# Row sums of a fused attention and feed-forward kernel moved directly behind the value product, with one more warm-up matmul

## The chip, the cores and the metric

One core of one Trainium2 chip. The metric is the device time of one execution in microseconds (us), a median over runs. The kernel before takes 463.5 us (three runs, 463.35 to 464.38). TensorE multiplies matrices into PSUM, ScalarE computes exponentials and other functions, VectorE does elementwise arithmetic, GpSimd prepares inputs and issues loads, SyncE issues transposing transfers and stores. Single executions scatter: 35 runs of the kernel before in one set lay between 461.23 and 467.68 us. So most numbers below are durations inside a profile, and whole times are compared over many runs.

## The reference

Attention over 8 batches, 12 heads, 448 positions and 64 columns, followed by a gated feed-forward block over 3584 tokens:

```python
scores = scale * np.matmul(q, k.transpose(0, 1, 3, 2))
scores = scores - np.max(scores, axis=-1, keepdims=True)
attn = np.exp(scores)
attn = attn / (np.sum(attn, axis=-1, keepdims=True) + 1e-09)
x = np.matmul(attn, v)          # -> (3584, 768)
g = x @ w_gate                  # (768, 1536)
silu = g * (1.0 / (1.0 + np.exp(-g)))
out = silu * (x @ w_val) @ w_out
```

## The kernel before

It works through the heads in pairs and weaves attention and feed-forward into **visits**. A visit computes three score chunks of a pair (`s`), one or two products of an earlier pair of pairs (`acc`: the row sums, or one half of the value product), the small last score chunk (`sr`), and then a share of the feed-forward work of an earlier batch (`gp` and `vp`, a gate and a value projection; `op`, the output projection). A PSUM buffer is free again when its **reader**, the engine that takes the result out, is done. Every `acc`, `sr`, `vp` and `op` takes its PSUM buffer from one pool, `ps_f`, of **two** buffers, in turn; `s` and `gp` take theirs from `ps_s`, with three.

```python
ps_s = ctx.enter_context(tc.tile_pool(name="ps_s", bufs=3, space=PSUM))
ps_f = ctx.enter_context(tc.tile_pool(name="ps_f", bufs=2, space=PSUM))
...
def scaled(p0, t, acc):                     # reader of a value product
    ...
    nc.vector.tensor_tensor(X[kk][...], acc[:, 0:S], R[p0][:], ALU.mult)

def sums(p0, wide=False):                   # row sums: E times a matrix of ones
    if wide:
        acc = ps_s.tile([128, 2, 512], FP32, tag="s", name="acc")[:, 0]
    else:
        acc = ps_f.tile([128, 512], FP32, tag="f", name="acc")
    ...
def recips(p0, acc):                        # reader of the row sums
    ...
    nc.vector.tensor_copy(ssb[:], acc[:, 0:S])
    return [...]                            # four reciprocals, issued later one by one
...
def mm(dst, lhsT, rhs, start, stop):        # feed-forward matmul
    if not tiled[0]:
        nc.tensor.matmul(dst, lhsT=lhsT, rhs=rhs, start=start, stop=stop)
        return
    for j in range(4):                      # four pieces of 32 columns: the form of the products
        nc.tensor.matmul(dst[ts(j, 32), :], lhsT=lhsT[:, ts(j, 32)], rhs=rhs, ...)
...
def product(kind, p0):
    if kind == "sums":
        pop_deferred(99)
        deferred.extend(recips(p0, sums(p0)))
    else:
        pop_deferred(99)
        scaled(p0, kind, pv(p0, kind))
```

In the loop over visits, `todo` holds up to two products. Where it holds two, the first is the second half of a value product and the second the row sums of the next pair of pairs. The first is issued behind the scores; the sums come behind `sr` (early blocks) or behind the visit's `gp`,`vp` pairs (later blocks), except in a visit that opens a new block, where both come together.

The softmax here doesn't subtract the row's maximum and nothing guards it: scores larger than these inputs give would overflow.

Of the kernel before, what the change touches and what calls it, by code (L numbers as in the profile page):

```python
# [23 lines left out]
TILED = 8  # L24
# [4 lines left out]
def kernel(  # L29
# [72 lines left out]
    def dummy(n):  # L102
        wp = ps_f.tile([128, 512], FP32, tag="f", name="wp")
        for _ in range(n):
            nc.tensor.matmul(wp[:], lhsT=warm[:, 0:128], rhs=warm[:], start=True, stop=True)
# [40 lines left out]
    def load_v(g):  # L146
        b = g // GPB
        heads = ds((g % GPB) * 2 * GP, 2 * GP)
        v16[g] = raws.tile([128, 2 * GP * NC * D], FP16, tag="vt", bufs=3, name="vt")
        if g * GP < FULL:  # L150
            nc.gpsimd.dma_start(v_old(g), v[b, heads].rearrange("h (p c) d -> p h (c d)", c=NC))
            return
        nc.gpsimd.memset(v_rest(g), 0.0)  # L153
        nc.gpsimd.dma_start(v_main(g), v[b, heads, 0:SM].rearrange("h (p c) d -> p h (c d)", c=3))
        for hx in range(2):
            nc.gpsimd.dma_start(
                v_rest(g)[ts(hx, SR), :, hx],
                v[b, heads, SM:].rearrange("(i t) p d -> t p i d", t=2)[hx],
            )
# [14 lines left out]
    def prep(pr):  # L174
        if pr >= FULL:
            rq, km, kr = raw[pr]
            qk16 = attp.tile([128, 2, NC, 2, D], FP16, tag="qk16", bufs=3, name="qk16")
            nc.gpsimd.memset(qk16[96:128, 1], 0.0)
            nc.gpsimd.memset(qk16[:, 0, 3], 0.0)
            nc.gpsimd.tensor_copy(qk16[:, 0, 0:3].rearrange("p c h d -> p h c d"), km)  # L180
            for hx in range(2):
                nc.gpsimd.tensor_copy(qk16[ts(hx, SR), 0, 3, hx], kr[ts(hx, SR)])
            nc.gpsimd.tensor_copy(qk16[0:P, 1].rearrange("p c h d -> p h c d"), rq)
            qkT[pr] = attp.tile([128, 2 * NC, 128], FP16, tag="qkT", name="qkT", bufs=5)
            nc.sync.dma_start_transpose(
                qkT[pr][:], qk16[:].rearrange("p t c h d -> p (t c h d)")
            )
            return None
        rq, rk = raw[pr]
        if pr == 0 or pr >= NPE:  # L190
            qk16 = attp.tile([128, 2, NC, 2, D], FP16, tag="qk16", bufs=3, name="qk16")[0:P]
            for t, src in enumerate((rq, rk)):
                dst = qk16[:, 1 - t].rearrange("p c h d -> p h c d")
                if pr == 0:
                    nc.vector.tensor_copy(dst[:, 0], src[:, 0])
                    nc.scalar.activation(dst[:, 1], src[:, 1], AF.Copy)
                else:
                    nc.gpsimd.tensor_copy(dst, src)
        qkT[pr] = attp.tile([128, 2 * NC, 128], FP16, tag="qkT", name="qkT", bufs=5)
        qkT[pr] = qkT[pr][:].rearrange("p c q -> p (c q)")[:, 0 : 2 * NC * P].rearrange(  # L200
            "p (c q) -> p c q", q=P
        )
        if pr >= NPE:
            nc.sync.dma_start_transpose(
                qkT[pr], qk16.rearrange("p t c h d -> p (t c h d)")
            )
            return None

        def turn0():
            for t in range(2):  # L210
                tp = ps_s.tile([128, 2, 512], FP32, tag="s", name="tp")
                for c in range(NC):
                    for hx in range(2):
                        nc.tensor.matmul(
                            tp[ts(hx, 64), c // 2, ds(c % 2 * P, P)],
                            lhsT=qk16[:, 1 - t, c, hx],
                            rhs=ident[:],
                            start=True,
                            stop=True,
                        )  # L220
                dst = qkT[pr][:, ts(1 - t, NC)].rearrange("p (a c) q -> p a (c q)", a=2)
                nc.vector.tensor_copy(dst[:, 0], tp[:, 0, 0 : 2 * P])
                nc.scalar.activation(dst[:, 1], tp[:, 1, 0 : 2 * P], AF.Copy)

        def turn():
            if pr < FIRST + 2:
                tp = ps_s.tile([128, 2 * NC, 256], FP16, tag="s", name="tp")
            else:
                tp = ps_f.tile([128, 2 * NC, 128], FP16, tag="f", name="tp")
            for t in range(2):  # L230
                for c in range(NC):
                    for hx in range(2):
                        src = raw[pr][t][:, hx, c, :]
                        nc.tensor.transpose(tp[ts(hx, 64), (1 - t) * NC + c, 0:P], src, ident[:])
            nc.vector.tensor_copy(qkT[pr], tp[:, :, 0:P])

        return turn if pr else turn0
# [92 lines left out]
    def recips(p0, acc):  # L330
        ssb = attp.tile([128, S], FP32, tag="ssb", bufs=1)
        nc.vector.tensor_copy(ssb[:], acc[:, 0:S])
        rt = R[p0]
        return [
            lambda i=i: nc.vector.reciprocal(rt[:, ts(i, P)], ssb[:, ts(i, P)]) for i in range(4)  # L335
        ]
# [6 lines left out]
    tiled = [False]  # L343
# [94 lines left out]
    with tc.manual_schedule():  # L438
# [10 lines left out]
        load_qk16(4)  # L449
        load_v(0)  # L450
        load_v(1)
        dummy(6)
        prep(0)()
        dummy(1)
        turn = prep(1)
# [21 lines left out]
        def pop_deferred(n=1):  # L477
            for _ in range(n):
                if deferred:
                    deferred.pop(0)()  # L480
# [82 lines left out]
        for p0 in range(FIRST, NPAIR, 2):  # L563
            x = done[p0 + 1] + 1
            step = 2 if x < len(visits) and len(visits[x]) == 2 else 1
            queue += [(x, "sums", p0), (x + step, 0, p0), (x + step + 1, 1, p0)]
        while len(plan) < len(visits) or queue:
            x = len(plan)
            todo = []
# [3 lines left out]
        adds = {0: 0}  # L573
# [5 lines left out]
# [8 lines that stand above are left out]
        carry = 0.0  # L587
        for x, (chunks, todo) in enumerate(plan):
            for pr, c in chunks:
                qk(pr, c)  # L590
            end = min([y for y in adds if y > x] + [len(plan) + 1])
            if x == 0:
                for t in range(2):
                    scaled(p4, t, halves[t])
                add_block(0, end)
            turn2 = None
            entered = [pr for pr, c in chunks if c == 0]
            for pr in entered:
                if NPE <= pr + 3 < NPAIR:
                    prep(pr + 3)  # L600
                if pr % 2 == 0 and 14 <= pr + LA < NPAIR:
                    load_qk16(pr + LA)
            for pr, c in chunks:
                if c == 2 and pr < NPE - 2:
                    prep(pr + 2)()
            if x in adds and x > 0:
                while todo:
                    product(*todo.pop(0)[1:])
                add_block(adds[x], end - x)
            elif todo:  # L610
                product(*todo[0][1:])
            for pr in entered:
                if (pr + 2) % GP == GP - 1 and 4 <= (pr + 2) // GP + 1 < NGRP:
                    load_v((pr + 2) // GP + 1)
                for w in wq.pop(pr, []):
                    emit(w)
            tiled[0] = bool(todo or x in adds) and (not chunks or chunks[0][0] >= TILED)
            for pr in entered:
                if pr >= FULL:
                    qk_rest(pr)  # L620
            if adds[max(y for y in adds if y <= x)] < 2:
                for item in todo[1:]:
                    product(*item[1:])
                carry = run_budget(left() / (end - x) + carry)
            else:
                at, n = count["at"], count["visits"]
                no = share(count["o"], at, n)
                nf = 1
                if no and count["more"] > 0:
                    o_left = sum(1 for y in range(at, n) if share(count["o"], y, n))  # L630
                    extra = -(-count["more"] // o_left)
                    nf += extra
                    count["more"] -= extra
                count["at"] += 1
                for y in range(nf):
                    if fvq:
                        run_fv()
                for item in todo[1:]:
                    product(*item[1:])
                for _ in range(no):  # L640
                    run_o()
            tiled[0] = False
# [36 lines left out]
```

## Time and profile before

| | before |
|---|---|
| median of three runs | 463.49 us |
| span of the profiled run | 463.2 us |
| TensorE busy | 97% |
| VectorE, ScalarE, GpSimd busy | 52%, 49%, 40% |
| groups of row sums | 24, of which 13 stand late (12 in visits, 1 in the tail) and are what the change moves |

In the lines of the profile, `E` are the exponentials, `ones` the matrix of ones, `X` a finished value product, `ssb` VectorE's copy of the row sums, `sg`, `t` and `hts` the steps from `gp` and `vp` to the input of `op`, and `wp` the warm-up matmuls, whose results nobody reads. A form such as `128*32` is the part of TensorE's array that one matmul uses (rows by columns); going from one form to another is a change of the tiling mode. An "issue" hole is idle time for which the profile shows no wait.

The prediction below shows the shares, TensorE's waits and a late visit of the later blocks. Two more views matter. The first is TensorE's timeline in an early block (start us, duration us, engine, line, operation, result<-operands, forms, count, and in brackets the idle time before with its releaser):

```profile
99.56 0.94 PE L284 MATMUL acc<-E,vt 128*32 128x448 f16 x16
100.33 0.36 PE L350 MATMUL sr<-qkT 128*32 128x448 f16 x4
101.24 0.94 PE L284 MATMUL acc<-E,ones 128*32 128x448 f16 x16 [0.54 <-DVE X L311]
...
107.29 0.78 PE L260 MATMUL s<-qkT 64*128 64x448 f16 x6
```

With two buffers, the third user in a row needs the buffer of the first: the sums wait until VectorE has read the value product (`X`). The second view is VectorE in the late visit that the prediction shows:

```profile
207.83 0.69 DVE L381 SCALAR_TENSOR_TENSOR hts<-t,vp 128x512 f16<-128x512 f32 x1
208.46 0.62 DVE L332 COPY ssb<-acc 128x448 f32<-128x448 f32 x1
```

`hts`, the reader of the last `vp`, ends at 208.52, and `op`, which needs that `vp`'s buffer, starts at 208.57. That is the repeated hole of 0.16 us.

### The profile page before, as it was taken

To read this page: it belongs to the slowest core of one execution; us is meant where nothing else is said; L and a number is where in the kernel's file an instruction comes from. 1 tells how busy PE (TensorE), PEld (TensorE's weight loads), DVE (VectorE), ACT (ScalarE), POOL (GpSimd) and SP (SyncE) were. 2 spreads that over 40 slices of the span, in tenths; PEclk is the share of its full clock that TensorE was granted. 3 is DMA by queue.
4 is the path that set the end of the run, shared out by engine and by line. 5 is a ranking of instruction groups with operands and counts; after the bars stand their busy time and mean duration, and the time that the engine had idled before them with its cause. 6 is when DMAs were issued, how large, how long until landed. Compare 5 with 4: busy or idle time off the path is not lost.

```text
span 463.2 us, 17335 instructions
## 1 busy us (share of the span) xinstructions
PE 449.4 (97%) x7843; PEld 247.7 (53%) x7843; DVE 238.8 (52%) x375; ACT 225.9 (49%) x353; POOL 184.3 (40%) x380
## 2 busy tenths in 40 slices
PE   8899999999999999999998999999999999999996
PEld 3345555544456655555555656555556666544564
DVE  2665754557773653646645527446366366355200
ACT  5986666555546445444554464445544642222222
POOL 8454825996975064910849018450230000000000
PEclk9999999999999999999999999999999999999999
DMA  9999999999798638990859558963342101200133
GB/s 137 196 201 200 186 178 126 185 167 148 88 99 113 83 45 130 121 120 3 120 92 98 95 83 116 105 62 81 60 55 59 37 3 38 69 0 2 34 103 102
DMA packets 99146, 45.62 MB, mean 98 GB/s; under 512 B 69888, under 2 KB 95616, under 8 KB 99072
## 3 DMA queue, kind: packets, MB, share of 16 engines
q0 software_dynamic: 54848, 23.37, 42.6%
q1 hardware_dynamic: 44128, 21.09, 26.7%
q8 instruction: 61, 1.00, 0.9%
q14 instruction: 13, 0.11, 0.1%
q10 hardware_dynamic: 96, 0.05, 0.0%
HBM read 47.19 MB, written 11.01 MB: 126 GB/s over the span
## 4 chain that ended last, share of the span: by engine, by line
PE 88%; DVE 5%; ACT 3%; issue 1%; DMA 1%; SPq 0%; DVEq 0%; ACTq 0%
PE gp L350 18%; PE op L350 18%; PE vp L350 16%; PE acc L284 11%; PE s L260 7%; PE op L347 6%; PE gp L347 5%; PE vp L347 5%; ACT E L263 2%; DVE t L378 2%; PE sr L350 2%; DVE hts L381 1%; ACT sg L366 1%; DVE R L335 1%; DMA rk<-in_k_dram 1%
## 5 line engine op out<-in xcount | busy, mean ns | idle before, releaser
L263 ACT ACTIVATE E<-s 128x896 f16<-128x896 f32 (+1 forms) x156 | 131.5, 923 | 13.9 <-PE s L260 13.7
L378 DVE SCALAR_TENSOR_TENSOR t<-sg,gp 128x384 f32<-128x384 f32 (+1 forms) x96 | 59.0, 615 | 90.1 <-ACT sg L366 90.0
L350 PE MATMUL vp<-X,wv 128*32 128x384 f16 (+1 forms) x1824 | 99.5, 351 | 1.6 <-issue 1.6
L350 PE MATMUL gp<-X,wg 128*32 128x384 f16 (+1 forms) x1824 | 99.2, 351 | 0.0
L366 ACT ACTIVATE sg<-gp 128x384 f32<-128x384 f32 (+1 forms) x96 | 53.4, 557 | 89.2 <-PE gp L350 63.9
L411 ACT ACTIVATE osb<-op 128x384 f32<-128x384 f32 (+1 forms) x57 | 27.6, 484 | 126.9 <-PE op L350 103.1
L350 PE MATMUL op<-wo,hts 128*32 128x384 f16 x1968 | 86.6, 326 | 2.9 <-issue 0.9
L350 PEld LDWEIGHTS <-hts 128*32 128x32 f16 x1968 | 56.0, 97 | 30.9 <-issue 6.4
L335 DVE RECIPROCAL R<-ssb 128x112 f32<-128x112 f32 x92 | 71.4, 820 | 0.8
L350 PEld LDWEIGHTS <-wv 128*32 128x32 f16 x1824 | 50.3, 97 | 37.6 <-issue 2.5
L350 PEld LDWEIGHTS <-wg 128*32 128x32 f16 x1824 | 50.8, 97 | 34.7
L311 DVE TENSOR_TENSOR X<-acc,R 128x448 f16<-128x448 f32 x48 | 29.7, 624 | 73.2 <-PE acc L284 70.8
L381 DVE SCALAR_TENSOR_TENSOR hts<-t,vp 128x384 f16<-128x384 f32 (+1 forms) x96 | 59.6, 621 | 11.9 <-PE vp L350 1.3
L153 POOL MEMSET vt<- 128x384 f16 x12 | 5.0, 419 | 113.3 <-PE acc L284 113.3
L284 PE MATMUL acc<-E,vt 128*32 128x448 f16 (+1 forms) x768 | 45.2, 355 | 0.0
L260 PE MATMUL s<-qkT 64*128 64x448 f16 x312 | 41.8, 358 | 1.8 <-ACT E L263 1.3
L347 PE MATMUL op<-wo,hts 128*128 128x384 f16 (+1 forms) x192 | 29.6, 316 | 0.0
L284 PEld LDWEIGHTS <-vt 128*32 128x32 f16 (+1 forms) x768 | 16.8, 96 | 23.0 <-issue 14.7
L347 PE MATMUL gp<-X,wg 128*128 128x512 f16 (+1 forms) x120 | 26.7, 358 | 0.2 <-DVE t L378 0.2
L347 PE MATMUL vp<-X,wv 128*128 128x512 f16 (+1 forms) x120 | 26.6, 358 | 0.0
L260 PEld LDWEIGHTS <-qkT 64*128 64x128 f16 x312 | 12.0, 94 | 27.2 <-issue 21.8
L284 PE MATMUL acc<-E,ones 128*32 128x448 f16 (+1 forms) x384 | 22.6, 353 | 2.1 <-DVE X L311 1.7
(53 smaller groups left out, 325.7 us busy)
## 6 DMA issues: line engine op xcount, KB each, us to landing
q<-in_q_dram POOLq DMA_DIRECT2D x22, 224.0 KB, 5.8
k<-in_k_dram POOLq DMA_DIRECT2D x18, 192.0 KB, 6.6
vt<-in_v_dram POOLq DMA_DIRECT2D x12, 288.0 KB, 7.0
out_dram<-osb SPq DMA_DIRECT2D x7, 336.0 KB, 3.2
wg<-in_moe_w_gate_dram POOLq DMA_DIRECT2D x8, 288.0 KB, 11.1
wv<-in_moe_w_val_dram POOLq DMA_DIRECT2D x8, 288.0 KB, 11.4
wo<-in_moe_w_out_dram POOLq DMA_DIRECT2D x2, 1152.0 KB, 18.6
out_dram<-osb SPq DMA_DIRECT2D x8, 288.0 KB, 3.1
```

The costliest lines, as they stand in the source:

```text
L153: nc.gpsimd.memset(v_rest(g), 0.0)
L260: nc.tensor.matmul(s[:, hx, 0:S], lhsT=lhsT, rhs=rhs, start=True, stop=True)
L263: nc.scalar.activation(dst, s[0:m, :, 0:S], AF.Exp, scale=sm_scale)
L284: nc.tensor.matmul(acc[ts(j, 32), 0:S], lhsT=weights(pr, hx, c), rhs=rhs, start=(c == 0), stop=(c == NC - 1),)
L311: nc.vector.tensor_tensor(X[kk][:, hp + t, ts(bb, S)], acc[:, 0:S], R[p0][:], ALU.mult)
L335: lambda i=i: nc.vector.reciprocal(rt[:, ts(i, P)], ssb[:, ts(i, P)]) for i in range(4)
L347: nc.tensor.matmul(dst, lhsT=lhsT, rhs=rhs, start=start, stop=stop)
L350: nc.tensor.matmul(dst[ts(j, 32), :], lhsT=lhsT[:, ts(j, 32)], rhs=rhs, start=start, stop=stop)
L366: nc.scalar.activation(sg[:, 0:n], gp[:, 0:n], AF.Tanh, scale=0.5)
L378: nc.vector.scalar_tensor_tensor(t1[:, 0:n], sg[:, 0:n], 1.0, gp[:, 0:n], ALU.add, ALU.mult)
L381: nc.vector.scalar_tensor_tensor(hts[:, fb, 0:n], t1[:, 0:n], 0.5 * HS, vp[:, 0:n], ALU.mult, ALU.mult)
L411: nc.scalar.activation(osb[:, ds(m0, w)], op[:, 0:w], AF.Copy, scale=1.0 / HS)
```

## The change

The intent, as the words of the change have it: both products of a visit stand directly behind its scores, so that the switch from feed-forward matmuls to products and back happens once per visit; and TensorE gets a seventh warm-up matmul at the start, before its first transposes.

```diff
-        dummy(6)
+        dummy(7)
         prep(0)()
@@
+            any_p = len(todo)
             if x in adds and x > 0:
                 while todo:
                     product(*todo.pop(0)[1:])
                 add_block(adds[x], end - x)
-            elif todo:
-                product(*todo[0][1:])
+            while todo:
+                product(*todo.pop(0)[1:])
@@
-            tiled[0] = bool(todo or x in adds) and (not chunks or chunks[0][0] >= TILED)
+            tiled[0] = bool(any_p) and (not chunks or chunks[0][0] >= TILED)
@@
             if adds[max(y for y in adds if y <= x)] < 2:
-                for item in todo[1:]:
-                    product(*item[1:])
                 carry = run_budget(left() / (end - x) + carry)
@@
                     if fvq:
                         run_fv()
-                for item in todo[1:]:
-                    product(*item[1:])
                 for _ in range(no):
                     run_o()
```

## The prediction

> **What bounds the kernel now.** I read the page first: engine shares, the 40 slices, the chain that ended last.
>
> ```profile
> PE 449.4 (97%) x7843; PEld 247.7 (53%) x7843; DVE 238.8 (52%) x375; ACT 225.9 (49%) x353; POOL 184.3 (40%) x380
> ...
> PE   8899999999999999999998999999999999999996
> ...
> PE 88%; DVE 5%; ACT 3%; issue 1%; DMA 1%; SPq 0%; DVEq 0%; ACTq 0%
> ```
>
> TensorE is busy in every slice and holds 88% of the chain; the others are half idle. Except in the first 25 us, where ScalarE's exponentials run without a break from 9.48 us to 24.5 us, the time is the sum of the matmuls plus the small holes between them. So a reordering can only win or lose holes. TensorE's own waits name them:
>
> ```profile
> PE acc L284 <- DVE X L311: 1.7, 3, 0.6
> PE vp L350 <- issue: 1.6, 2, 1.3
> ...
> PE op L350 <- issue: 0.9, 1, 0.9
> PE op L350 <- DVE hts L381: 0.7, 4, 0.2
> ```
>
> The three waits of `acc` and the four of `op` each name a reader that had not emptied a PSUM buffer. I then read TensorE's timeline (start us, us, ...), visit by visit. Three consecutive visits of one block give the whole argument; a visit runs from one `s` to the next:
>
> ```profile
> 182.03 0.74 PE L260 MATMUL s<-qkT 64*128 64x448 f16 x6
> 182.70 0.94 PE L284 MATMUL acc<-E,vt 128*32 128x448 f16 x16
> 183.47 0.93 PE L284 MATMUL acc<-E,ones 128*32 128x448 f16 x16
> 184.37 0.37 PE L350 MATMUL sr<-qkT 128*32 128x448 f16 x4
> ...
> 191.81 0.74 PE L260 MATMUL s<-qkT 64*128 64x448 f16 x6
> ...
> 200.67 0.74 PE L260 MATMUL s<-qkT 64*128 64x448 f16 x6
> ...
> 206.18 1.47 PE L350 MATMUL vp<-X,wv 128*32 128x512 f16 x24
> 207.48 0.93 PE L284 MATMUL acc<-E,ones 128*32 128x448 f16 x16
> 208.57 2.13 PE L350 MATMUL op<-wo,hts 128*32 128x384 f16 x48 [0.16 <-DVE hts L381]
> 210.64 0.55 PE L260 MATMUL s<-qkT 64*128 64x448 f16 x4
> ```
>
> The first visit already has the order of the change: the value product, then the row sums (`acc<-E,ones`), then the rest. It takes 191.81-182.03 = 9.78 us. The second has no sums and takes 8.86 us. The third has the same work as the first, but its sums stand behind two `gp`,`vp` pairs: 210.64-200.67 = 9.97 us. So the early place costs 0.92 us and the late one 1.11 us. That comparison, made on the chip in the kernel before, is the core of the forecast.
>
> **What the Trainium skill says.** "Perfetto Trace Analysis", section Optimization Strategy (under Identifying Performance Opportunities), reads the same gap, repeated on the engine that should be saturated, as a possible lack of SBUF or PSUM for the next tile. The trace agrees: 0.16 us appears four times and 0.54 to 0.57 us three times. "TensorEngine Tiling (Array Packing)", section Key Properties, says that changing the tiling mode drains TensorE. If that were the gain, it would be nil here: products and, in these visits, the feed-forward matmuls all have the form 128*32; `vp` to sums starts 207.48-206.18 = 1.30 us apart, as `gp` to `vp` does (206.18-204.89 = 1.29). "TensorE: Matmul & The Clock Gate", Part 1, gives 426.7 ns for 512 columns on the cold array; the first warm-up loads follow each other at 0.42 to 0.43 us, which agrees. "Runtime: NRT & Kernel Launch", section Instruction fetch mechanics, says that instructions come in blocks of 256 (16 KiB) by DMA, mostly hidden; the page shows 61 packets, 1.00 MB, on the instruction queue, and 15,688 TensorE instructions / 256 = 61.3. I take the three "issue" holes (1.31, 0.88, 0.33 us, all inside a group or where no buffer was awaited) for late blocks, which is an inference.
>
> **The change part by part.** The listing of the changed program's order settles what moves. Apart from one matmul, TensorE's instructions are the same in number and form; ScalarE, GpSimd and SyncE keep their order. Of 24 sums groups, 13 move; the other 11 already stand directly behind the value product or belong to the first part. In every moved case it is the sums that come forward; no value product moves.
>
> 1. Four visits with 512 columns and 48 `op` (200.67, 219.50, 312.10, 330.93): 9.97 each now, 9.78 in the early order. Cause: the `f` buffers are two. Late, the sums take the buffer of the first `vp` and the first `op` needs that of the second, whose reader `hts` ends at 207.83+0.69 = 208.52; the sums fill only 0.75 us of that wait. Early, the two `op` candidates are free. Gain 4 x 0.19 = 0.76.
> 2. Five visits with 384 columns (145.69, 163.86, 256.06, 274.23, 365.85): for example 172.49-163.86 = 8.63, against 138.11-129.61 = 8.50 early. Gain 5 x 0.13 = 0.65.
> 3. Two visits of the block without `op` (98.89, 114.24): 107.29-98.89 = 8.40 and 122.66-114.24 = 8.42, against 91.43-83.61 = 7.82 early. Here the late order is value product, `sr`, sums, and the sums wait for the buffer whose reader X is only just starting. Early, the sums take the other buffer and their 0.75 us of matmuls cover most of X; `sr` waits about 0.13 us instead (183.47 to 184.37 is 0.90, where 0.77 is a group's usual pitch). Gain 2 x 0.59 = 1.18.
> 4. The visit at 71.66: sums wait 0.57 for X, then `op` 0.21 for `sr`'s exponential. Early, sums at 73.10, `sr` after X (73.35+0.62) at about 74.0; then `op` waits for the copy of the sums, which VectorE starts after X and ends at about 74.75. `op` at about 74.8 instead of 75.18: gain 0.4. A new wait eats part of it.
> 5. The tail, 384.67: `op` at 385.71 is 1.04 behind the sums' start, 0.75 being their work. Early gain 0.29.
>
> Sum of 1 to 5: 0.76+0.65+1.18+0.4+0.29 = 3.3 us. All of it lies on the path, since TensorE is the path from about 25 us on.
>
> 6. The seventh warm-up matmul: the first six finish streaming at 1.20+6x0.427 = 3.76; the seventh streams until 4.19. The first transposes start at 4.09, when VectorE's cast is ready, so they slip 0.1 us; but their second half waits for another input (the cast that starts at 4.50) until 4.85. Cost 0 to 0.1, which I put at +0.1. Warmth could pay, as `s` at 8.88 is still slow (four in 0.93) and those at 11.52 fast (two in 0.36); I choose nothing for it.
>
> 463.49 - 3.3 + 0.1 = 460.3 us.
>
> **The rivals.** (a) **VectorE becomes late.** Early sums bring a copy of 0.62 and four reciprocals of 0.82 between the `t` and `hts` of the two pairs: 3.9 us beside 2 x 1.38 = 2.8, so 6.7 us where two pairs take TensorE 4 x 1.30 = 5.2. If `vp`'s buffer were freed late, each of nine visits could lose 0.5 us: up to +4.5, ending at about 465. Against it: the visits at 129.61, 182.03, 238.33, 293.46 and 349.77 have just this order, and `gp`,`vp` step on there without a hole; the last reciprocal spills into the `op` stretch. (b) **Fewer mode changes**, the apparent intent: worth several us if each moved group had a drain at both ends; the pitches above speak against it. (c) **The warm-up turns the clock on a window earlier**: the exponentials wait 1.12 us before 9.48, of which perhaps 0.7 could go: 459.6. (d) **The gaps are hidden anyway**, because a freed TensorE waits for exponentials: ScalarE has idle stretches of 0.6 to 3.7 us in every such visit, so I see little of that; it would make 463.5. (e) **Late instruction blocks move**: the issue holes total 2.5 us[...]; +1 or -1.5.
>
> **Range and chances.** The counted gain rests on durations of the same sequence, so I trust it to about 0.7 us; fetch holes and start add about 1 us. The range is 458.8 to 462.6. A change of 2% is 9.3 us, three times what all counted holes hold, so within 2% gets 0.98, each side 0.01.
>
> **What would show it.** In the changed profile: the waits of `acc` for X gone; the four waits of `op` for `hts` gone; visits of 9.8, 8.5 and 7.8 us where 9.97, 8.63 and 8.4 stood; `sr` 0.90 behind the sums in 13 more visits; a wait of `op` for the copy of the sums in the visit at 71.66; VectorE's total unchanged. Wrong would be: waits of `vp` or `op` for `hts` or `ssb` in the moved visits (rival a), or other issue holes.

## The result

The changed kernel gives the right result. Its median is 460.97 us (four runs, 459.87 to 461.38) against 463.94 us for the kernel before beside it (four runs). The ratio is 0.9931, with a 95% interval of 0.9904 to 0.9957. Ratios here are the mean time of one kernel's fast runs over that of the other's fast runs of the same rounds, so not quite the ratio of the medians. Two repeats on other occasions gave 0.9931 and 0.9932.

The page of the changed kernel, the lines that answer to those of before (engine shares; TensorE's busy tenths; the chain that ended last):

```profile
PE 446.9 (97%) x7844; PEld 250.2 (54%) x7844; DVE 238.6 (52%) x375; ACT 226.8 (49%) x353; POOL 184.3 (40%) x380
...
PE   8899999999999999999999999899999999999996
...
PE 93%; DVE 3%; ACT 2%; issue 1%; DMA 1%; SPq 0%; DVEq 0%; ACTq 0%
```

The chain is TensorE's to 93% instead of 88%: the steps through VectorE and ScalarE fell from 8% to 5%. TensorE's waits:

```profile
PE op L350 <- issue: 2.6, 1, 2.6
...
PE vp L350 <- issue: 1.1, 1, 1.1
...
PE op L350 <- DVE ssb L332: 0.4, 1, 0.4
```

The three waits of `acc` for `X` and the four of `op` for `hts` no longer appear. The forecast wait for the copy of the sums is there, once. The "issue" holes have grown from 2.5 to 3.7 us. The visit that answers to the late one of before (200.67 there):

```profile
196.88 0.74 PE L260 MATMUL s<-qkT 64*128 64x448 f16 x6
197.55 0.94 PE L284 MATMUL acc<-E,vt 128*32 128x448 f16 x16
198.32 0.93 PE L284 MATMUL acc<-E,ones 128*32 128x448 f16 x16
199.22 0.37 PE L350 MATMUL sr<-qkT 128*32 128x448 f16 x4
...
203.29 1.48 PE L350 MATMUL vp<-X,wv 128*32 128x512 f16 x24
204.59 2.14 PE L350 MATMUL op<-wo,hts 128*32 128x384 f16 x48
206.66 0.74 PE L260 MATMUL s<-qkT 64*128 64x448 f16 x6
```

It takes 9.78 us, and `op` starts 1.30 us behind `vp` without a hole. Going through all visits from one `s` to the next, before against after, only the moved ones and those with an issue hole differ by more than 0.02 us:

| part of the run | before to after, us |
|---|---|
| start, up to 68.16 us of before | -1.48 |
| visit at 71.66 | -0.42 |
| two visits of the early block (98.89, 114.24) | -0.56, -0.57 |
| five visits with 384 columns | -0.14, -0.11, -0.13, -0.11, -0.14 |
| four visits with 512 columns | -0.19, -0.17, -0.19, -0.17 |
| tail, to the next value product | -0.27 |
| three visits with issue holes (91.43, 246.83, 282.86) | -0.52, -0.34, +1.85 |
| span 463.2 to 459.6 | -3.6 |

So this pair of profiles gained 3.17 us from the moved sums, 1.48 us at the start, which I had not counted, and gave 0.99 us back in holes whose waits the profile cannot name. Were the start and the holes parts of the change, or chance? Theory: the moved sums gain 3.2 us by PSUM buffers, and the rest is chance (theory C of the expectations). Rivals: the place behind the value product pays in itself, by fewer changes of the tiling mode; the seventh warm-up matmul makes TensorE fast earlier and pays for part of it (theory B); the new order makes the issue holes longer.

### The profile page after: what moved, and what is told of

Its sections match the earlier page's. It is cut to its first block, busy times and chain, and to the rows that moved or that the text cites. A ratio compares the mean times of both kernels' runs of the same rounds, so it can differ in the third digit from the quotient of the medians.

```text
span 459.6 us, 17337 instructions
## 1 busy us (share of the span) xinstructions
PE 446.9 (97%) x7844; PEld 250.2 (54%) x7844; DVE 238.6 (52%) x375; ACT 226.8 (49%) x353; POOL 184.3 (40%) x380
## 4 chain that ended last, share of the span: by engine, by line
PE 93%; DVE 3%; ACT 2%; issue 1%; DMA 1%; SPq 0%; DVEq 0%; ACTq 0%
PE vp L350 18%; PE gp L350 18%; PE op L350 18%; PE acc L284 13%; PE s L260 7%; PE op L347 6%; PE gp L347 5%; PE vp L347 5%; PE sr L350 2%; ACT E L263 1%; DVE R L335 1%; DMA rk<-in_k_dram 1%; PE tp L234 0%; DVE ssb L332 0%; DVE X L311 0%
## 5 line engine op out<-in xcount | busy, mean ns | idle before, releaser
L335 DVE RECIPROCAL R<-ssb 128x112 f32<-128x112 f32 x92 | 73.9, 831 | 0.8
L350 PEld LDWEIGHTS <-wv 128*32 128x32 f16 x1824 | 51.7, 97 | 35.2 <-issue 1.5
L350 PEld LDWEIGHTS <-wg 128*32 128x32 f16 x1824 | 51.9, 97 | 32.6
L347 PEld LDWEIGHTS <-hts 128*128 128x128 f16 x192 | 18.4, 98 | 11.1
```

The lines of the kernel that those rows point to most:

```text
L335: lambda i=i: nc.vector.reciprocal(rt[:, ts(i, P)], ssb[:, ts(i, P)]) for i in range(4)
```

## The experiments

### Each half of the change alone

The seventh warm-up matmul alone, on the kernel before:

```diff
-        dummy(6)
+        dummy(7)
```

> The kernel before with the seventh warm-up matmul and nothing else. Theory A (my prediction's term 6): no gain, 0 to +0.1 us, about 464. Theory B (the changed kernel's profile, where the matmuls are fast from about 5.2 us on and the work at 68 us stands 1.5 us earlier): [...]1.0 to 1.5 us faster, about 462.5, in all or nearly all runs. Theory C: [...]the runs scatter over 1.5 us for six and for seven matmuls alike and the means agree.

The new order alone, the changed kernel with `dummy(6)`:

> The changed order with six warm-up matmuls. Counting theory: the visits of the moved sums shorten by 0.11 to 0.19 (nine), 0.57 (two), 0.42 (one) and 0.29 (the tail), in all 3.2 us, so about 460.8 if the instruction holes are as in the kernel before. If the seventh matmul carries 1.5 us of the measured 3 us, this run gains only 1.5 to 2 us unless the holes differ (theory: the larger hole of the changed kernel, 2.60 against 0.88 us, comes with the order).

Measured, on one chip: warm-up alone 463.93 us median against 463.98, ratio 1.0003 (0.9981 to 1.0024). The order alone 462.69 us, ratio 0.9966 (0.9946 to 0.9987), which is 1.6 us faster. A second set of the same kernel, with the edit repeated in a later call, had this expectation:

> The changed order tiled with six warm-up matmuls, again, now on one chip with the changed kernel. It was 1.9 us faster than before at a clock of 0.998 or more where the visits count 3.2. Theory B: its missing 1.3 us are late clocks that six matmuls leave to chance; it is about 1 us slower than the changed kernel beside it. Theory C: equal to the changed kernel within the scatter of 1.2 us a run.

It gave 461.63 us, ratio 0.9942 (0.9922 to 0.9963). So the order alone is faster. Both means, 1.6 and 2.7 us, lie below the 3.2 us that its visits count, though only the first interval excludes 3.2, and though in the profiles the moved visits were as short as in the changed kernel (in the first, 7.83, 10.45, 9.78). The matmul alone shows no gain. Both repeats of the whole change gave more than the order alone:

> The changed kernel once more, for a second profile and more runs on the chip of the others. Counting theory: the visits repeat to 0.02 us (9.78, 8.50, 7.84), and only the start and the instruction holes differ; at a granted clock of 0.998 or more it is 2 to 3 us faster than before, as the changed order with six warm-up matmuls (1.9) within the noise. If the seventh matmul matters, it is over 1 us faster than that run was.

> The changed kernel beside the run with six warm-up matmuls. About 460.6, as twice before; Theory B puts it 1 us below that run, Theory C at the same time. A third profile of its instruction holes: at the same places (visits near 243 and 278) or none, of 0.2 to 2.6 us.

They gave 460.76 us, ratio 0.9931 (0.9906 to 0.9956), and 461.22 us, ratio 0.9932 (0.9910 to 0.9955). Two of the last kernel's 19 runs were far off (517.4 and 1618.5 us), were marked slow and do not count. One source of scatter can be set apart: in the first set of the order alone, 7 of 22 runs had a mean granted clock of 0.995 or 0.996 and were 2.1 us longer than the others, where the kernel before beside it had 3 of 35 such runs. Without such runs, the means are 1.9 and 2.8 us below the kernel before for the order alone, 3.3 us both times for the whole change, and 0.0 for the warm-up alone. Even so, the intervals of all runs overlap, and at this scatter the parts cannot be separated by time.

### Buffers or place: the sums in the other pool

Both orders, with one edit: the sums of the main loop take a buffer of `ps_s`.

```diff
-                deferred.extend(recips(p0, sums(p0)))
+                deferred.extend(recips(p0, sums(p0, True)))
```

The order of before:

> The order of before; only the PSUM buffer of the row sums is taken from the three-buffer pool of the scores, in the main loop. Buffer theory: the late place costs nothing by itself, the two-buffer pool does; each sums group then costs its 0.75 us of matmuls wherever it stands (visits of 9.97 become about 9.6, 8.63 become 8.35, 8.40 become 7.7), some 5 to 6 us faster than before, about 458.5. Position theory (being directly behind the value product is what pays, or a mode change): no change, about 463.9.

The order of the change:

> The changed order and the sums in the pool of the scores. Buffer theory: the wait of 0.13 to 0.17 us of the small score matmul behind the sums goes, in some 20 visits, 3 us faster than the changed kernel, about 457.8, and within 0.5 us (apart from the warm-up) of the run with the late order in that pool. If the exponentials free the score buffer too late, the sums wait instead, up to 0.3 us each, and it is no faster than the changed kernel. Position theory: as the changed kernel, about 461.

Measured, beside the same runs of before: late 459.29 us, ratio 0.9884 (0.9847 to 0.9921); early 457.63 us, ratio 0.9877 (0.9838 to 0.9917). A late visit in that pool:

```profile
198.08 0.74 PE L260 MATMUL s<-qkT 64*128 64x448 f16 x6
...
203.59 1.47 PE L350 MATMUL vp<-X,wv 128*32 128x512 f16 x24
204.88 0.93 PE L284 MATMUL acc<-E,ones 128*32 128x448 f16 x16
205.64 2.12 PE L350 MATMUL op<-wo,hts 128*32 128x384 f16 x48
207.70 0.55 PE L260 MATMUL s<-qkT 64*128 64x448 f16 x4
```

It takes 9.62 us, 0.76 more than one without sums (8.86), which is the sums' own work; `op` follows 0.76 us behind them. The same stretch with the early order in that pool:

```profile
197.39 0.94 PE L284 MATMUL acc<-E,ones 128*32 128x448 f16 x16
198.14 0.38 PE L350 MATMUL sr<-qkT 128*32 128x448 f16 x4
```

Here `sr` starts 0.75 us behind the sums instead of 0.90, and the visit takes 9.66 us. So, in the tiled kernel, where the sums stand no longer matters once they leave the pool of two: late is even 0.04 us a visit better. **What the moved sums gained was a better rotation through two buffers.** The place theory is out. The two medians alone would not show this, since the early kernel also has the seventh warm-up matmul; the visits do, and both profiles have the same fast start (see below). Against the changed kernel I had expected 3 us; the ratios, 0.9877 and 0.9931, are about 2.5 us apart. One new wait takes part of it: in the visit at about 61 us, the sums wait 0.6 us for an exponential that must free a score buffer (that visit took 6.15 us instead of 5.53).

### Without tiling: mode changes, and a quieter kernel

The feed-forward matmuls of all visits in one piece of 128 columns, so that each passage between them and the products changes the tiling mode:

```diff
-TILED = 8
+TILED = 99
```

The order of before, six warm-up matmuls:

> The order of before with the feed-forward matmuls of all visits in one piece of 128 columns instead of four of 32. Mode theory (what the change seems to be for): the sums behind the feed-forward pairs now stand between two changes of the tiling mode, so a late sums visit costs about 0.2 us more against a visit without sums than in the tiled kernel (1.11 becomes 1.3). Fetch theory: TensorE's instructions fall from 15,688 to about 7,000, some 27 blocks instead of 61, so the issue holes (1.2 to 3.7 us in the profiles so far) mostly go. Against before: the added changes cost about 0.1 us each, four per visit more, in some 30 visits, so up to 6 us slower, less 2 us of holes.

The changed order, seven:

> The changed order without the tiling. Mode theory: early sums share the mode changes of the value product, so the visits of the moved sums shorten by 0.2 us more than in the tiled kernels: nine by 0.3 to 0.4, and the whole gains 5 us on the late order untiled. If a change of mode costs nothing, the gain is the 3.2 us of the buffers again.

Late: 464.66 us, ratio 1.0013 (1.0000 to 1.0026). Early: 459.08 us, ratio 0.9901 (0.9875 to 0.9926). TensorE's timeline of a late visit, and then of the sums and `sr` in the early kernel:

```profile
201.55 0.74 PE L260 MATMUL s<-qkT 64*128 64x448 f16 x6
202.22 0.94 PE L284 MATMUL acc<-E,vt 128*32 128x448 f16 x16
203.09 0.36 PE L347 MATMUL sr<-qkT 128*128 128x448 f16 x1
...
207.18 1.46 PE L347 MATMUL vp<-X,wv 128*128 128x512 f16 x6
208.56 0.94 PE L284 MATMUL acc<-E,ones 128*32 128x448 f16 x16
209.54 2.11 PE L347 MATMUL op<-wo,hts 128*128 128x384 f16 x12
211.58 0.74 PE L260 MATMUL s<-qkT 64*128 64x448 f16 x6
```

```profile
199.12 0.93 PE L284 MATMUL acc<-E,ones 128*32 128x448 f16 x16
200.02 0.35 PE L347 MATMUL sr<-qkT 128*128 128x448 f16 x1
```

A visit without sums changes the mode once more than a tiled one, before `sr`, and takes 8.97 us instead of 8.86: that change costs 0.11 us where nothing hides it. (`sr` starts 0.87 us behind the value product, 0.77 in the tiled kernel. A visit with late sums changes the mode three times more; the four that I had expected everywhere were too many.) A moved visit gains 0.26 to 0.28 us (10.03 to 9.75) where it gained 0.17 to 0.19 tiled. I had expected 0.2 more; it is 0.09 more, and not by the two changes around the late sums. From `vp` to `op` the late visit takes 2.36 us here and 2.39 tiled: in both, `op` starts 0.05 us after `hts` ends (209.49 here, 208.52 there), so both changes lie inside that wait. Against a visit without sums, late sums cost 1.06 us here and 1.11 tiled, early ones 0.78 and 0.92, so the 0.09 us come from the early side: `sr` starts 0.90 us behind the sums with a mode change and without, so the change that every other visit pays for is hidden in the wait for a buffer. Over all moved visits the untiled order gains 3.97 us and 0.27 in the tail, 4.24 together. The intended saving, fewer switches, shows in neither kernel: tiled, there are none to save, and untiled, those around the late sums cost nothing beside the wait. What they would cost in the late order with the sums in the other pool was not run.

The instruction queue of the late kernel's page (packets, MB, share of 16 engines):

```profile
q8 instruction: 29, 0.48, 0.4%
```

It moves 29 packets, where the tiled kernels move 61, and no untiled profile has an issue hole of TensorE. The scatter falls with it: the six runs of the early order lie within 0.6 us. The last combination, early and untiled with the sums in the other pool:

> The changed order, sums in the pool of the scores, without tiling: the three effects together. If the holes go and a mode change costs about 0.1 us: 3 us faster than the changed order untiled, and within 2 us of the tiled run with the sums in that pool (457.6).

It gave 459.20 us, ratio 0.9902 (0.9876 to 0.9927), the same as without that pool. My 3 us did not come. In the trace, `sr` starts 0.87 us behind the sums: with the buffer wait gone, the mode change is no longer hidden. The wait for an exponential came back too (6.25 us instead of 5.55 in its visit).

### The warm-up, in the kernel that is quiet enough

The late untiled kernel's 22 runs fall into two groups, 7 runs at 463.2 to 463.5 us and 15 at 464.5 to 464.9. The late order with seven warm-up matmuls:

> The late order untiled with seven warm-up matmuls. The untiled runs scatter by only 0.2 us within a group, and with six the late order fell into two groups, 7 runs at 463.2 to 463.5 and 15 at 464.5 to 464.9. Theory B (the seventh matmul lets the clock rise in time): all runs, or nearly all, at 463.4. Theory C[...]: again two groups, most runs at 464.7.

The early order with six:

> The changed order untiled with six warm-up matmuls; with seven, six runs of six were at 458.8 to 459.4. Theory B: two groups, 459.1 and some 1.4 us higher at 460.5, most runs in the higher. Theory C: the same groups as with seven. The order itself then gives, lower group against lower group, 463.35 - 459.1 = 4.25 us.

With seven, 20 of 22 late runs are at 463.2 to 463.8 (median 463.54) and two at 464.4 and 464.8. With six, all six early runs are at 460.3 to 460.4, where all six with seven were at 458.8 to 459.4. So there are two starts that differ by 1.3 us: with six matmuls most runs get the slow one, with seven hardly any. That is read off the times; the four profiles, one of each kernel, fit their groups. The early untiled kernel with six:

```profile
8.45 0.61 PE L105 MATMUL wp<-warm 128*128 128x512 f16 x1
8.99 0.62 PE L260 MATMUL s<-qkT 64*128 64x448 f16 x4
```

The late untiled kernel with seven:

```profile
6.70 0.39 PE L105 MATMUL wp<-warm 128*128 128x512 f16 x1
7.02 0.39 PE L234 MATMUL tp<-ident,q 112*64 112x112 f16 x8
```

A warm-up matmul of 512 columns takes 0.61 us while TensorE is slow and 0.39 when it is fast. (The profile's granted clock is 1.00 in both, so this shows in durations alone.) With seven, TensorE is fast by 6.70 us; with six, in this run, it is still slow at 8.45. The slow start delays the scores, and ScalarE, which bounds the first 25 us, idles 1.00 us between its second and third exponential, until 9.47. Order alone, group against same group: 464.7 - 460.37 = 4.3 us (slow start) and 463.37 - 459.08 = 4.3 us (fast start), against 4.24 counted in the visits. Here the count is confirmed to a tenth.

The tiled profiles have the same two starts: all five with seven matmuls are fast, and of the four with six, two are slow (the kernel before and the second set of the order alone) and two fast. So the seventh matmul can act there too, but nine profiles do not give its mean worth.

### What stays open: the issue holes

In the tiled kernels TensorE sometimes stops in the middle of a group, with every buffer free. The largest hole of the changed kernel, by stretches (us, TensorE busy, weight loads, VectorE, ScalarE, GpSimd, clock, DMA share, GB/s), and then TensorE's first wait in its third profile:

```profile
284.00:287.00 3.00, 2.76 (x69) 1.60 (x60) 0.56 (x1) 0.49 (x1) 0.00 (x0) 1.00 1.52 138
287.00:289.00 2.00, 0.00 (x0) 0.00 (x0) 0.00 (x0) 0.00 (x0) 0.00 (x0) 1.00 0.05 3
```

```profile
PE op L350 <- issue: 2.9, 1, 2.9
```

All engines stand still, and so do the transfers, right behind a burst of them. The totals of these holes, one number per profile: late order 2.5 and 1.2; early order 3.7, 1.7, 4.0, 2.0, 3.7; sums in the other pool 2.2 (late) and 1.8 (early). In the pool of two, the early order's mean is 3.0 against 1.9, but two profiles of one order and five of the other, with this scatter, don't show that the order causes it. That the holes belong to the number of TensorE instructions is better supported, since they vanish when that number falls to half, though untiling changes the matmuls' form too. Runs with a mean granted clock of 0.995 or 0.996, some 2 to 3.5 us longer, occurred only in tiled kernels, never in the 62 untiled runs; why, no run here shows.

## Why the prediction was right

The prediction said 460.3 us and 458.8 to 462.6; three sets measured 460.97, 460.76 and 461.22. Its mechanism held; that its total came so close is partly luck.

- **The main step holds: a visit's early and late form can be read off the kernel before.** Its five terms were 0.76, 0.65, 1.18, 0.4 and 0.29; the changed profile has 0.72, 0.63, 1.13, 0.42 and 0.27, in all 3.17 instead of 3.3. The untiled pair confirms such a count in time.
- **The cause of these terms holds.** The rotation through two PSUM buffers made the holes: in the other pool the late order loses them too.
- **Rival (a), a late VectorE, did not come.** In the visit at 196.88, the copy and the first reciprocal (199.30 to 200.81) ran before the first `t`, where VectorE had been idle, and only two reciprocals stood between the pairs. No `vp` or `op` waits for `hts`.
- **Rival (b), fewer mode changes, had nothing to work on** in the tiled kernel. Untiled, the changes around the late sums were hidden too.
- **Rival (d), a freed TensorE that waits for exponentials, did not come:** 3.17 us of the 3.3 arrived in the visits. The sign of `sr` 0.90 us behind the sums came in 12 more visits (0.90 to 0.93), not 13: the tail has no `sr`.
- **Term 6 was wrong: the seventh warm-up matmul was put at +0.1 us.** The step that failed is the effect of the start: the term counted the slip of the transposes and left out that TensorE becomes fast earlier. In the quiet kernel the slow start, 1.3 us longer, came in 15 of 22 runs with six in one order and 6 of 6 in the other, and with seven in 2 of 22 and none of 6. Rival (c) had it, at 0.7 us, but the sum chose nothing for it.
- **Rival (e), the holes that no wait explains, went against the gain**: +0.99 us in this pair, inside the range I gave it.

That is the luck: the last two, -1.48 and +0.99 us in this pair of profiles, were both left out of the sum and partly cancel. The range covered them; the sum did not foresee them. (A slip without effect: 15,688 TensorE instructions is the changed kernel's count; the page of before has 15,686.) For the tiled kernels the share of each in the time is not settled: warm-up alone showed no gain (1.0003, and the interval still allows 0.9 us).

The runs also point to a better version: the changed kernel with the sums in `ps_s` ran at 457.63 us, ahead of both kernels.

## What to carry to other kernels

Look for a visit that already has the wanted order, in the kernel that you have, and compare its start-to-start time with that of its neighbours; this told five terms to 0.05 us each. When a group waits for a buffer, ask which of the pool's users came that many places before it: moving one user, or giving it another pool, may be worth the same, and the pool is the simpler cure. When runs scatter more than the effect, make a variant without the source of the scatter (here half the instructions) and measure there.

## What the Trainium skill lacked or had wrong

- "TensorE: Matmul & The Clock Gate", Part 1, tells of about 3.4 us of sustained activity and says that the start is run-variable. It does not say how much idle time that stretch may hold. Here six warm-up matmuls (to 3.76 us by reckoning, then 0.3 to 0.5 us idle in the profiles) left 15 of 22 runs with the slow start, all of 6 in the other order; seven (to 4.19 us, then 0.1 us idle) left 2 of 22 and none of 6. A slow start cost 1.3 us, the seventh matmul 0.43 us of work. Whether the gap or the shorter stretch decides, no run here shows.
- "TensorEngine Tiling (Array Packing)", Key Properties, says that a mode change drains TensorE but has no size. Here it was 0.11 us where nothing hid it, and nothing where a wait for a buffer (0.13 us early; `hts` late) ended later.
- "Runtime: NRT & Kernel Launch", Instruction fetch mechanics, calls block boundaries mostly hidden. With 61 packets on the instruction queue the profiles lost 1.2 to 4.0 us in unexplained issue holes, once 2.9 us in one; with 29 packets none. That the fetch causes them is likely, not shown.
- "Perfetto Trace Analysis", Matmuls, asks that independent groups rotate through PSUM banks. No page says that in a shared pool of two the order of the users decides: the same sums cost a visit 0.92 us in one place, 1.11 in another, and 0.76 to 0.80 in a pool of three.
